# Scores of the first four attention pairs: one head's 128 queries, with 64-row matmuls for each half of the keys

## The chip, the cores and the metric

The kernel runs on one NeuronCore of a Trainium2 chip. The metric is the device time of one execution in microseconds (us); lower is better. A profile is one execution taken by the hardware profiler. Its engines are PE (TensorE matmuls), PEld (TensorE weight loads), DVE (VectorE), ACT (ScalarE), POOL (GpSimd) and SP (SyncE, which here only issues DMAs).

## What is computed

A sparse softmax attention (4 batches, 8 heads, 576 positions, head size 64) is followed by two feed-forward blocks on 2304 tokens. Everything is float32 at the borders.

```python
def _attn_ref(q, k, v, tau):                      # q, k, v: (4, 8, 576, 64)
    scale = 1.0 / np.sqrt(q.shape[-1])
    scores = scale * np.matmul(q, k.transpose(0, 1, 3, 2))
    thresh = np.max(scores, axis=-1, keepdims=True) - tau
    scores = np.where(scores >= thresh, scores, -1000000000.0)
    scores = scores - np.max(scores, axis=-1, keepdims=True)
    attn = np.exp(scores)
    attn = attn / (np.sum(attn, axis=-1, keepdims=True) + 1e-09)
    return np.matmul(attn, v)
# x = attention output as (2304, 512)
# moe:  (x @ w1) * (x @ w2) @ w3 @ w_out          # d_ff 1024
# moe2: elu(x @ w_in) @ w_out2                    # d_ff 2048
```

## The kernel before

The 32 heads are worked on as 16 pairs, and each pair as nine tiles of 128 query rows, 144 tiles in all. One tile passes through these steps: scores on PE (`emit_S`) into an `s` buffer of two PSUM banks (288 keys in each), the row maximum on DVE (`emit_max`), two tiny POOL steps for bias and threshold, the exponential on ACT (`emit_exp`), mask and row sum on DVE (`emit_mask`). Then the probabilities are transposed. Most tiles of the first four pairs do this on PE (`emit_X`, five transposes back into the same `s` buffer) with a copy by ACT (`emit_C`) into `pt`; other tiles are split into two float16 parts (`emit_H`, `emit_L`) and go through DMA transposes (`emit_T`). There are three `s` buffers, so a tile's scores wait until an earlier tile has left its buffer. The product with V (`emit_PV`) follows per group of four or five tiles, then the normalisation, for which the reciprocal row sums take a way through DRAM (`store_r`, `load_r`).

The first four pairs (`NPL = 4`, tiles 0 to 35) form their scores in plain float32; the later ones split operands into two fast float32 parts. In the plain pairs a tile holds 64 queries of the even head and 64 of the odd head. Both heads lie in one `qkp` buffer, the even one on rows 0 to 63, the odd one on rows 64 to 127, and the opposite rows of the query columns are zeros, written once by `new_plain` (eight memsets on DVE and POOL). The four matmuls of a tile contract all 128 rows with 64 stationary columns: two heads by two halves of the keys. A profile shows two records for each plain float32 matmul.

While attention runs, PE also works on the first products of the feed-forward block (`ab`), one block of 576 tokens behind, with weights that DVE, ACT and POOL unpack (`raw_w`, `u_w`, `w_w`, `W`). The order of all this is made by a planner (`Plan`): each step has an engine, a written-in duration, a key and what it depends on, and the planner simulates engines and emits each engine's instructions in the order it found. `d` in the loop over tiles is the duration of a tile's scores. On the chip each engine works in exactly that order. From about 460 us on, only feed-forward work is left, in an order that is written out by hand and untouched here.

Of the kernel before, what the change touches and what calls it, by code (L numbers as in the profile page):

```python
# [7 lines left out]
F32 = mybir.dt.float32  # L8
# [10 lines left out]
P = 128  # L19
B, H, S, D = 4, 8, 576, 64  # L20
HS = S // 2
# [123 lines left out]
def attention_moe_moe2(  # L145
# [106 lines left out]
    QW = S + D  # L252
    qkt, raw = {}, {}

    def new_plain(p, low, high):
        t = hp_.tile([P, 1792], F32, tag=f"qk{p % 2}", name=f"qkp{p}", bufs=2)
        qkt[2 * p] = qkt[2 * p + 1] = t
        low.memset(t[D:P, :S], 0.0)
        high.memset(t[:D, S:2 * S], 0.0)

    def load_plain(p, j, eng=SP):
        r = slice(j * D, (j + 1) * D)
        t = qkt[2 * p][r, j * S:3 * S].rearrange("p (x c) -> p x c", c=S)
        eng.dma_start(t[:, ::2 - j], qk[2 * p + j][r].rearrange("p (x c) -> p x c", c=S))

    def load_qk(h):
        raw[h] = rqk.tile([P, 2 * S], F32, tag="rqk", name=f"rqk{h}")
# [73 lines left out]
    def emit_S(i):  # L341
        sc[i] = s = ps_s.tile([P, 2, 512], F32, tag="s", name=f"s{i}")
        if i >= NTILE:
            return
        p, pos = SEQ[i]
        j, t = ORDER[pos]
        a, b = qkt[2 * p], qkt[2 * p + 1]
        if p < NPL:
            for n in range(2):
                k = 2 * S + n * HS  # L350
                for j, c in enumerate((pos * D, S + (pos + 1) % TPP * D)):
                    T.matmul(s[j * D:(j + 1) * D, n, :HS], a[:, c:c + D], a[:, k:k + HS], start=True, stop=True)
            return
        if j == 2:
            ops = [(a[:, 4 * P:5 * P], a), (b[:, :P], b)]
        elif j == 1:
            ops = [(b[:, (t + 1) * P:(t + 2) * P], b)]
        else:
            ops = [(a[:, t * P:(t + 1) * P], a)]
        ops = [(q, k, QW + x * S) for q, k in ops for x in range(2)]  # L360
        for n in range(2):
            for x, (q, k, c) in enumerate(ops):
                c += n * HS
                T.matmul(s[:, n, :HS], q, k[:, c:c + HS], start=(x == 0), stop=(x == len(ops) - 1))  # L364
# [50 lines left out]
    def place(i):  # L415

        p, pos = SEQ[i]
        j, t = ORDER[pos]
        o = pt[p, int(pos >= 4)]
        if p < NPL:  # L420
            c = (pos - 4 * (pos >= 4)) * P
            return o.rearrange("p c j t -> p c (j t)")[:, :, c:c + P]
        if j == 2:
            return o[:, :, :, 256:320]
        c = (t % 2) * P
        return o[:, :, j, c:c + P]

    def emit_T(i):
        p, pos = SEQ[i]
        if p >= NPL and ORDER[pos][0] == 2:  # L430
            for j in range(2):
                SP.dma_start_transpose(pt[p, 1][:, :, j, 256:320], hl[i][j * D:j * D + D, :])
        else:
            SP.dma_start_transpose(place(i), hl[i])
# [32 lines left out]
    def store_r(p, n):  # L467
        w = 4 + n
        rdr[p, n] = rdp.tile([w, P], F32, tag=f"rd{n}", name=f"rd{p}_{n}")
        if p < NPL:  # L470
            d = rdr[p, n].rearrange("t c -> (t c)").rearrange("(j t c) -> t j c", j=2, c=D)
            SP.dma_start(d, rts[p, n][:w].rearrange("t (j c) -> t j c", j=2))
        else:
            SP.dma_start(rdr[p, n], rts[p, n][:w])

    def load_r(p, n, k):
        if k == 0:
            rbc[p, n] = rbp.tile([P, 320], F32, tag="rb", name=f"rb{p}_{n}")
        o = rbc[p, n]
        if p < NPL:  # L480
            d = rdr[p, n].rearrange("t c -> (t c)").rearrange("(j o c) -> j o c", j=2, o=1)
            SP.dma_start(o[:, :NW[n]], d.to_broadcast([2, D, NW[n]]))
        elif k == 0:
            d = rdr[p, n][:4].rearrange("t c -> (t c)").rearrange("(j o c) -> j o c", j=2, o=1)
            SP.dma_start(o[:, :256], d.to_broadcast([2, D, 2 * P]))
        else:
# [5 lines left out]

    def emit_PV(p, n, part):
        w, q = NW[n], pt[p, n]
        if p < NPL:
            q = q.rearrange("p c j t -> p c (j t)").rearrange("p c (t j d) -> p c j t d", j=2, d=D)
        if part == 0:
            po_[p, n] = ps_m.tile([P, 512], F32, tag="m", name=f"pv{p}_{n}")
        if not of_dma(p, n):
            k = min(P, S - part * P)  # L500
            for j in range(2):
                T.matmul(  # L502
                    po_[p, n][j * D:(j + 1) * D, :w], vraw[p][:k, j, part * D:(part + 1) * D],
                    q[:k, part, j, :w // D if p < NPL else w], start=(part == 0), stop=(part == 4),
                )
            return
        for c, x, vc in PVC[part]:
            for j in range(2):
                x_ = q[:, c, j, :w // D if p < NPL else w]
                T.matmul(  # L510
                    po_[p, n][j * D:(j + 1) * D, :w], v16[p][:, j, x, vc * D:(vc + 1) * D], x_,
                    start=(c == 0 and x == 0), stop=(c == 8),
# [61 lines left out]


    V.memset(spread, 1.0 / VSCALE)
    for p in range(NPL):
        new_plain(p, *((V, G), (G, G), (V, V), (V, V))[p])
    for j, e in enumerate((SP, A)):
        load_plain(0, j, e)  # L580
    SP.dma_start(tau_sb, tau.to_broadcast([P, 1]))
# [20 lines left out]

    for i in range(NTILE + 4):
        p, pos = SEQ[i] if i < NTILE else (NPAIR - 1, 0)
        d = 0.05 if i >= NTILE else 1.15 if p < NPL else 1.1 if pos == 8 else 0.6
        o = S_[i] = op(call(emit_S, i), eng="PE", us=d, key=i)
        ring["s", i] = take("s", 3, o)
        if i >= NTILE:
# [40 lines left out]
    for p in range(NPL):  # L649
        QK[p] = []  # L650
        if p:
            QK[p] = [op(call(load_plain, p, j), (), "SP", 0.1, AT[p, 0] - 8, 4.0) for j in range(2)]
        for i in range(NTILE):
            if SEQ[i][0] == p:
                pl.after(S_[i], *QK[p])
# [42 lines left out]

    GRP = sorted(((p, n) for p in range(NPAIR) for n in range(2)), key=lambda g: AT[g[0], 8 if g[1] else 3])
    def load_rs(p, n):  # L700
        for k in range(1 + (n and p >= NPL)):
            load_r(p, n, k)

    pvs = []
# [438 lines left out]
```

## Time and profile before

| | us |
|---|---|
| median of three runs | 1067.16 (1064.76 to 1068.95) |
| the profiled execution, its own time | 1067.07 |
| its span, first to last instruction | 1065.0 |
| PE busy in the span | 1014.1 |
| DVE busy in the span | 583.6 |

The profile's page gives busy time by engine, then 40 equal slices of the span with the busy share of each engine in tenths. A grouped view gives, for each line of code and shape, the busy time, the mean duration of one and the idle time of that engine just before, with what ended it ("<-DVE e L394" is a wait that VectorE's line 394 ended). The view of the waits sums who waited for whom. A timeline lists instructions in order, neighbours of a kind merged.

### The profile page before, as it was taken

The page shows a single profiled execution, that of the slowest core. Times are in us where ns is not written, and L with a number is a line of the kernel's source. Part 1 is how long each engine was busy: PE and PEld are TensorE (multiplying, and loading weights), DVE is VectorE, ACT ScalarE, POOL GpSimd, SP SyncE. Part 2 cuts the span into 40 slices and gives each one's busy share as a digit, 9 for nine tenths or more (in the row PEclk, how much of TensorE's full clock was granted, in tenths as well). Part 3 has the DMA queues.
Part 4 walks back from the last instruction along what each step waited for, and adds up shares of the span by engine and source line. Part 5 has one row for each costly group of instructions (what it writes and reads, how often), then busy time and mean ns, then how long its engine had stood idle before and what let it go on. Part 6 is the DMA issues. An engine that isn't in the chain of part 4 may idle for free.

```text
span 1065.0 us, 17060 instructions
## 1 busy us (share of the span) xinstructions
PE 1014.1 (95%) x6318; PEld 887.0 (83%) x6318; DVE 583.6 (55%) x1072; ACT 514.0 (48%) x864; POOL 441.7 (41%) x586
## 2 busy tenths in 40 slices
PE   7878999979999999989999999999999999999998
PEld 4445788867888888889879999989999899899997
DVE  4788888764676666646555565843332333323322
ACT  3776777764666665534334555533232232322322
POOL 1648867765657665413321231332222222222221
PEclk8999999998999999999999999999999999999999
DMA  8227688876559444466617673300000000000000
GB/s 264 90 92 197 133 159 137 138 151 158 112 129 160 122 116 87 102 211 211 218 45 242 190 239 110 119 1 30 1 1 30 1 30 1 2 30 1 30 1 30
DMA packets 119726, 109.70 MB, mean 103 GB/s; under 512 B 88176, under 2 KB 106844, under 8 KB 115036
## 3 DMA queue, kind: packets, MB, share of 16 engines
q1 hardware_dynamic: 115532, 78.97, 31.3%
q10 hardware_dynamic: 4112, 29.66, 8.1%
q8 instruction: 49, 0.80, 0.3%
q14 instruction: 33, 0.27, 0.1%
HBM read 73.73 MB, written 14.23 MB: 83 GB/s over the span
## 4 chain that ended last, share of the span: by engine, by line
PE 58%; DMA 1%; issue 1%; POOL 1%; ACT 1%; DVE 1%; SPq 0%; POOLq 0%; ACTq 0%; DVEq 0%
PE h L1033 19%; PE o L1062 19%; PE x L1000 9%; PE ab L552 6%; PE m L860 4%; DMA rb<-rd 1%; POOL hl L405 0%; PE s L364 0%; DMA th<-g_dr 0%; PE s L442 0%; PE pv L502 0%; PE pv L510 0%; DVE sl L200 0%; POOL hl L406 0%; ACT hl L401 0%
## 5 line engine op out<-in xcount | busy, mean ns | idle before, releaser
L552 PE MATMUL ab<-x,W 128*128 128x256 f32 (+1 forms) x1536 | 232.1, 301 | 3.5 <-DVE xf L521 3.5
L552 PEld LDWEIGHTS ab<-x,W 128*128 128x128 f32 x1536 | 211.0, 190 | 10.2 <-issue 3.8
L1062 PE MATMUL o<-WO,sl 128*128 128x512 f32 x864 | 215.7, 394 | 0.6 <-POOL sl L1054 0.6
L1033 PE MATMUL h<-sl,W 128*128 128x384 f32 x1152 | 215.7, 337 | 0.0
L1033 PEld LDWEIGHTS h<-sl,W 128*128 128x128 f32 x1152 | 202.8, 188 | 8.3
L1054 POOL TENSOR_TENSOR sl<-th,sl 128x384 fp32r<-128x384 f32 x87 | 88.4, 1017 | 266.5 <-ACT sl L1049 266.5
L1062 PEld LDWEIGHTS o<-WO,sl 128*128 128x128 f32 x864 | 161.1, 188 | 30.7 <-POOL sl L1054 1.1
L1042 DVE TENSOR_SCALAR th<-h 128x384 f32<-128x384 f32 x96 | 53.3, 555 | 182.8 <-PE h L1033 182.8
L394 DVE SCALAR_TENSOR_TENSOR e<-s,st,e 128x576 f32<-128x576 f32 x144 | 115.3, 814 | 59.2 <-ACT e L388 31.3
L1043 ACT ACTIVATE th<-th 128x384 f32<-128x384 f32 x96 | 50.4, 525 | 194.5 <-DVE th L1042 194.5
L373 DVE TENSOR_REDUCE st<-s 128x1 f32<-128x576 f32 x144 | 106.0, 748 | 23.5 <-PE s L364 7.3
L1000 PE MATMUL x<-sl,M 128*128 128x384 f32 x576 | 101.1, 337 | 0.5 <-ACT sl L199 0.3
L1000 PEld LDWEIGHTS x<-sl,M 128*128 128x128 f32 x576 | 99.6, 188 | 1.9 <-DVE sl L200 0.8
L405 POOL TENSOR_TENSOR hl<-e,hl 128x512 f16<-128x512 f32 x70 | 83.1, 1188 | 24.4 <-ACT hl L401 24.1
L364 PE MATMUL s<-qk 128*128 128x288 f32 x480 | 83.8, 307 | 8.4 <-DVE e L394 4.5
L388 ACT ACTIVATE e<-s,st 128x576 f32<-128x576 f32 x108 | 77.0, 736 | 27.2 <-DVE st L373 17.0
L1049 ACT ACTIVATE sl<-th 128x384 fp32r<-128x384 f32 x96 | 50.4, 525 | 76.7 <-PE o L1062 46.5
L1047 DVE SCALAR_TENSOR_TENSOR th<-th,h 128x384 f32<-128x384 f32 x96 | 53.1, 554 | 58.2 <-ACT th L1043 58.1
L364 PEld LDWEIGHTS s<-qk 128*128 128x128 f32 x480 | 70.1, 192 | 13.3 <-issue 3.8
L442 PE MATMUL s<-ident,e 128*128 128x128 f32 (+1 forms) x370 | 56.1, 284 | 19.5 <-DVE e L394 19.2
L446 ACT ACTIVATE pt<-s 128x640 f32<-128x640 f32 x74 | 51.5, 700 | 45.0 <-PE s L442 36.1
L442 PEld LDWEIGHTS s<-ident,e 128*128 128x128 f32 (+1 forms) x370 | 38.5, 136 | 37.4 <-DVE e L394 32.4
(89 smaller groups left out, 1200.4 us busy)
## 6 DMA issues: line engine op xcount, KB each, us to landing
rqk<-in_qk SPq DMA_DIRECT2D x24, 576.0 KB
raw_wo<-in_wo ACTq DMA_DIRECT2D x12, 1024.0 KB
th<-g_dr SPq DMA_DIRECT2D x48, 192.0 KB
raw_w<-in_w SPq DMA_DIRECT2D x8, 1024.0 KB
raw_w<-in_w3t ACTq DMA_DIRECT2D x8, 1024.0 KB
raw_win<-in_win ACTq DMA_DIRECT2D x8, 1024.0 KB
vr<-in_v SPq DMA_DIRECT2D x16, 320.0 KB
g_dr<-g SPq DMA_DIRECT2D x16, 320.0 KB
```

Of the source, the lines that this page charges most:

```text
L364: T.matmul(s[:, n, :HS], q, k[:, c:c + HS], start=(x == 0), stop=(x == len(ops) - 1))
L373: V.tensor_reduce(st[i][:, 0:1], sc[i][:, :, :HS], axis=AX.XY, op=ALU.max, negate=True)
L388: A.activation(et[i], sc[i][:, :, :HS], AF.Exp, bias=st[i][:, 2:3] if by_dma(i) else st[i][:, 0:1])
L394: V.scalar_tensor_tensor(et[i], sc[i][:, :, :HS], st[i][:, 1:2], et[i], op0=ALU.is_ge, op1=ALU.mult, accum_out=sm[p][:, pos:pos + 1],)
L405: G.tensor_tensor(t[:, S + 64:], e[:, :512], t[:, :512], op=ALU.subtract)
L442: T.transpose(o[:k, c * P:(c + 1) * P], e[:, c * P:c * P + k], ident)
L552: T.matmul(o[:, :w], wf[:, m, wx, kt, :], x[:, xx, :], start=(kt == 0 and k == 0), stop=(kt == NK - 1 and k == 2),)
L1000: T.matmul(o[:, :TB], M[:, f, mx, e * P:(e + 1) * P], gh[j, f][:, gx, :], start=(k == 0), stop=(k == 23),)
L1033: T.matmul(o[:, :TB], WI[f][:, wx, kt, :], xh[j, kt][:, xx, :], start=(k == 0), stop=(k == 3 * NK - 1),)
L1042: V.tensor_scalar(t, o[:, :TB], 0.0, None, op0=ALU.min)
L1054: (V if jobs else G).tensor_tensor(x[:, 1, :], thin[2 + f % 2], f32(x[:, 0, :]), op=ALU.subtract)
L1062: T.matmul(po[j, t], gg[j, f][:, gx, t * P:(t + 1) * P], WO[f // 2][:, f % 2, wx, :], start=(f == 0 and k == 0), stop=(f == NF2 - 1 and k ...
```

## The change

For the plain pairs each head now has its own half of the `qkp` buffer. Rows 0 to 63 hold its queries and the first 288 keys, rows 64 to 127 hold the same queries again and the last 288 keys. There are no zeros and no memsets. A tile is 128 queries of one head: two matmuls, each of 64 rows by 128 stationary columns, one on the upper and one on the lower rows, each into its own PSUM bank. The ninth tile of a pair holds the last 64 queries of both heads and takes four matmuls of 64 rows by 64 columns. Tile order, `pt` layout and reciprocals thereby become those of the later pairs. A head is loaded by three DMAs instead of one, and the second head's load of pairs 1 to 3 is planned behind the first head's. `load_r` takes a second DMA for the five-tile groups, and the ninth tile of pairs 1 and 3 takes two DMA transposes. The planner's duration of the scores becomes 0.66.

```diff
-    def new_plain(p, low, high):
-        t = hp_.tile([P, 1792], F32, tag=f"qk{p % 2}", name=f"qkp{p}", bufs=2)
-        qkt[2 * p] = qkt[2 * p + 1] = t
-        low.memset(t[D:P, :S], 0.0)
-        high.memset(t[:D, S:2 * S], 0.0)
     def load_plain(p, j, eng=SP):
-        r = slice(j * D, (j + 1) * D)
-        t = qkt[2 * p][r, j * S:3 * S].rearrange("p (x c) -> p x c", c=S)
-        eng.dma_start(t[:, ::2 - j], qk[2 * p + j][r].rearrange("p (x c) -> p x c", c=S))
+        if j == 0:
+            t = hp_.tile([P, 1792], F32, tag=f"qk{p % 2}", name=f"qkp{p}", bufs=2)
+            for x in range(2):
+                qkt[2 * p + x] = t[:, x * (S + HS):(x + 1) * (S + HS)]
+        t = qkt[2 * p + j]
+        for x in range(2):
+            r = slice(x * D, (x + 1) * D)
+            if x == 0:
+                eng.dma_start(t[r], qk[2 * p + j][r, :S + HS])
+            else:
+                eng.dma_start(t[r, :S], qk[2 * p + j][r, :S])
+                eng.dma_start(t[r, S:], qk[2 * p + j][r, S + HS:])
...
         if p < NPL:
-            for n in range(2):
-                k = 2 * S + n * HS
-                for j, c in enumerate((pos * D, S + (pos + 1) % TPP * D)):
-                    T.matmul(s[j * D:(j + 1) * D, n, :HS], a[:, c:c + D], a[:, k:k + HS], start=True, stop=True)
+            if j == 2:
+                ops = [(slice(0, D), a, 4 * P, D), (slice(D, P), b, 0, D)]
+            else:
+                ops = [(slice(0, P), (a, b)[j], t * P + j * D, P)]
+            for o, x, c, m in ops:
+                for n in range(2):
+                    r = slice(n * D, n * D + D)
+                    T.matmul(s[o, n, :HS], x[r, c:c + m], x[r, S:], start=True, stop=True)
...
     def emit_T(i):
-        if p >= NPL and ORDER[pos][0] == 2:
+        if ORDER[pos][0] == 2:
...
-        d = 0.05 if i >= NTILE else 1.15 if p < NPL else 1.1 if pos == 8 else 0.6
+        d = 0.05 if i >= NTILE else 0.66 if p < NPL else 1.1 if pos == 8 else 0.6
...
-            QK[p] = [op(call(load_plain, p, j), (), "SP", 0.1, AT[p, 0] - 8, 4.0) for j in range(2)]
+            QK[p] = [op(call(load_plain, p, 0), (), "SP", 0.1, AT[p, 0] - 8, 4.0)]
+            QK[p].append(op(call(load_plain, p, 1), QK[p][:1], "SP", 0.1, AT[p, 0] - 8, 4.0))
...
     def load_rs(p, n):
-        for k in range(1 + (n and p >= NPL)):
+        for k in range(1 + n):
             load_r(p, n, k)
```

On PE, at the scores of tiles 3 to 6 before (`s3` is tile 3's score buffer, `e3` its probabilities, `qkp1` the queries and keys of pair 1, `k` a filler product, `rr` the reciprocal sums):

```order
L352 MATMUL s3_217<-qkp0_117 64x288 x4
L352 MATMUL s4_226<-qkp1_120 64x288 x4
L442 MATMUL s2_171<-ident_114,e2_215 128x128 x4
L442 MATMUL s2_171<-ident_114,e2_215 64x128
L369 MATMUL k3_252<-spread_115 128x128 x2
L369 MATMUL k4_256<-spread_115 128x128 x2
L352 MATMUL s5_263<-qkp1_120 64x288 x4
L442 MATMUL s3_217<-ident_114,e3_250 128x128 x4
```

The same place on PE after the change:

```order
L359 MATMUL s3_220<-qkp0_117 128x288 x2
L446 MATMUL s2_165<-ident_114,e2_193 128x128 x4
L446 MATMUL s2_165<-ident_114,e2_193 64x128
L376 MATMUL k3_233<-spread_115 128x128 x2
L359 MATMUL s4_246<-qkp1_144 128x288 x2
L359 MATMUL s5_255<-qkp1_144 128x288 x2
L376 MATMUL k4_259<-spread_115 128x128 x2
L376 MATMUL k5_264<-spread_115 128x128 x2
L446 MATMUL s3_220<-ident_114,e3_244 128x128 x4
```

A tile's scores are two matmuls of 128 output rows in place of four of 64, and the scores of tile 4 stand behind the transposes of tile 2.

On SP, the loads behind pair 1 and the first weight piece before (`rqk` and `vr` are later queries, keys and values, `raw_w121` the second weight piece):

```order
L264 DMA qkp2_123<-in_qk 64x2x576
L264 DMA qkp2_123<-in_qk 64x1152
L264 DMA qkp3_126<-in_qk 64x2x576
L264 DMA qkp3_126<-in_qk 64x1152
L268 DMA rqk8_161<-in_qk 128x1152
L300 DMA vr1_196<-in_v5 128x640
L300 DMA vr2_234<-in_v5 128x640
L268 DMA rqk9_242<-in_qk 128x1152
L195 DMA raw_w121_261<-in_w12 128x2048
```

The later part of the same stretch on SP after the change, from `vr1` on:

```order
L303 DMA vr1_202<-in_v5 128x640
L264 DMA qkp1_144<-in_qk 64x864
L266 DMA qkp1_144<-in_qk 64x576
L267 DMA qkp1_144<-in_qk 64x288
L264 DMA qkp2_150<-in_qk 64x864
L266 DMA qkp2_150<-in_qk 64x576
L267 DMA qkp2_150<-in_qk 64x288
L264 DMA qkp3_154<-in_qk 64x864
L266 DMA qkp3_154<-in_qk 64x576
L267 DMA qkp3_154<-in_qk 64x288
L303 DMA vr2_242<-in_v5 128x640
L271 DMA rqk9_249<-in_qk 128x1152
```

The first heads of pairs 1 to 3 are still loaded ahead of `rqk8` and `vr1`; the second heads now stand behind `vr1` and ahead of `vr2`, `rqk9` and `raw_w121`, which is the next row.

On ACT, around the values of pair 1 and the second weight piece before (`v16` is made from `vr`, `u_w` from `raw_w`):

```order
L210 ACTIVATE u_w120_224<-raw_w120_155 128x1024
L305 ACTIVATE v16_1_237,am1_236<-vr1_196 128x2x320
L386 ACTIVATE e3_250<-s3_217,st3_232,esc_111 128x576
L446 ACTIVATE pt0_0_205<-s2_171 128x5x128
L446 ACTIVATE pt0_0_205<-s3_217 128x5x128
L232 ACTIVATE W0_286<-w_w120_239 128x2x512
L465 ACTIVATE rt0_0_297<-s5_263 4x128
L386 ACTIVATE e4_300<-s4_226,st4_283,esc_111 128x576
L305 ACTIVATE v16_3_312,am3_311<-vr3_274 128x2x320
L210 ACTIVATE u_w121_321<-raw_w121_261 128x1024
```

The same on ACT after the change:

```order
L210 ACTIVATE u_w120_229<-raw_w120_148 128x1024
L450 ACTIVATE pt0_0_201<-s2_165 128x5x128
L393 ACTIVATE e3_244<-s3_220,st3_231,esc_111 128x576
L308 ACTIVATE v16_1_253,am1_252<-vr1_202 128x2x320
L450 ACTIVATE pt0_0_201<-s3_220 128x5x128
L232 ACTIVATE W0_277<-w_w120_239 128x2x512
L469 ACTIVATE rt0_0_293<-s5_255 4x128
L393 ACTIVATE e4_296<-s4_246,st4_281,esc_111 128x576
L210 ACTIVATE u_w121_311<-raw_w121_262 128x1024
```

The copy of tile 2 and the exponential of tile 3 moved ahead of the step that needs `vr1`, and the step that needs `raw_w121` no longer stands behind the one that needs `vr3`.

## Rows read from the trace of the kernel before

**Rows 1.** The page, engines: busy us, share of the span, instructions.
```profile
PE 1014.1 (95%) x6318; PEld 887.0 (83%) x6318; DVE 583.6 (55%) x1072; ACT 514.0 (48%) x864; POOL 441.7 (41%) x586
```

**Rows 2.** Four stretches: length, busy us and count by engine, granted clock, DMA share, GB/s.
```profile
0.00:24.00 24.00, 16.39 (x93) 11.22 (x95) 12.06 (x27) 8.37 (x12) 4.66 (x16) 0.94 0.94 287
24.00:124.00 100.00, 87.21 (x639) 53.94 (x636) 81.58 (x152) 71.93 (x106) 68.21 (x101) 0.98 0.41 122
124.00:460.00 336.00, 311.88 (x2422) 271.64 (x2420) 228.42 (x505) 212.02 (x366) 211.00 (x356) 0.98 0.66 132
460.00:1065.00 605.00, 598.60 (x3168) 550.21 (x3168) 261.52 (x389) 221.72 (x381) 157.87 (x115) 1.00 0.23 77
```

**Rows 3.** PE by line in 24 to 124 us: busy, mean ns, idle before.
```profile
L352 PE MATMUL s<-qkp 128*64 128x288 f32 x244 | 36.1, 424 | 2.7 <-DVE e L394 1.4 <-ACT pt L446 1.1
L442 PE MATMUL s<-ident,e 128*128 128x128 f32 (+1 forms) x115 | 17.8, 289 | 9.8 <-DVE e L394 9.8
```

**Rows 4.** Timeline of PE: start, length, line, records, idle before.
```profile
6.02 5.40 PE L352 MATMUL s<-qkp 128*64 128x288 f32 x24 [2.04 <-DMA qkp<-in_qk]
...
22.54 2.19 PE L352 MATMUL s<-qkp 128*64 128x288 f32 x8 [4.10 <-ACT pt L446]
...
31.67 1.19 PE L352 MATMUL s<-qkp 128*64 128x288 f32 x8 [0.79 <-ACT pt L446]
...
34.98 2.16 PE L352 MATMUL s<-qkp 128*64 128x288 f32 x16
```

**Rows 5.** Timeline of PE in stretches of 0.05 us: the records that run there.
```profile
34.98 0.46 PE L352 MATMUL s<-qkp 128*64 128x288 f32 x2
...
35.27 0.41 PE L352 MATMUL s<-qkp 128*64 128x288 f32 x2
...
35.51 0.41 PE L352 MATMUL s<-qkp 128*64 128x288 f32 x2
```

**Rows 6.** The whole span by line and shape: busy, mean ns, idle before.
```profile
L552 PE MATMUL ab<-x,W 128*128 128x256 f32 x768 | 103.1, 285 | 0.0
...
L352 PEld LDWEIGHTS s<-qkp 128*64 128x64 f32 x288 | 19.9, 147 | 25.6 <-ACT pt L446 8.3 <-issue 7.3 <-DVE e L394 1.6
```

**Rows 7.** Waits in 24 to 124 us: total us, times, longest.
```profile
ACT pt L446 <- PE s L442: 8.7, 6, 3.5
...
DVE e L394 <- ACT e L386: 6.7, 11, 2.4
...
ACT pt L446 <- PE pv L502: 4.4, 1, 4.4
DVE st L373 <- PE s L352: 4.4, 6, 1.6
DVE st L373 <- PE s L460: 3.7, 3, 2.2
```

**Rows 8.** Timeline of the start: ACT and POOL where they wait for loads.
```profile
20.35 0.74 ACT L305 ACTIVATE v<-vr 128x640 f16<-128x640 f32 x1 [3.73 <-DMA vr<-in_v]
...
29.49 1.14 ACT L210 ACTIVATE u_w<-raw_w 128x1024 f32<-128x1024 f32 x1
...
19.64 0.74 POOL L271 TENSOR_SCALAR rqk<-rqk,esc 128x576 f32<-128x576 f32 x1 [6.72 <-DMA rqk<-in_qk]
```

**Rows 9.** DMAs in 0 to 30 us: 40 slices of 0.75 us, busy tenths, GB/s; issues.
```profile
DMA  0038999999988999999999999999998921000000
GB/s 0 0 55 240 270 220 199 379 308 212 272 227 328 415 380 312 232 209 237 243 258 209 313 328 401 413 462 435 369 485 378 391 115 53 20 7 0 0 3 0
...
qkp<-in_qk SPq DMA_DIRECT2D x7, 288.0 KB
...
qkp<-in_qk ACTq DMA_DIRECT2D x1, 288.0 KB
```

More of the change, by code (lines that the diff above doesn't have):

```diff
@@ L419, in place @@
         o = pt[p, int(pos >= 4)]
-        if p < NPL:
-            c = (pos - 4 * (pos >= 4)) * P
-            return o.rearrange("p c j t -> p c (j t)")[:, :, c:c + P]
         if j == 2:
@@ L469, in store_r @@
         rdr[p, n] = rdp.tile([w, P], F32, tag=f"rd{n}", name=f"rd{p}_{n}")
[L470 to L474, printed above, removed]
+        SP.dma_start(rdr[p, n], rts[p, n][:w])
     def load_r(p, n, k):
@@ L479, in load_r @@
         o = rbc[p, n]
[L480 to L483, printed above, removed]
+        if k == 0:
             d = rdr[p, n][:4].rearrange("t c -> (t c)").rearrange("(j o c) -> j o c", j=2, o=1)
@@ L494, in emit_PV @@
         w, q = NW[n], pt[p, n]
-        if p < NPL:
-            q = q.rearrange("p c j t -> p c (j t)").rearrange("p c (t j d) -> p c j t d", j=2, d=D)
         if part == 0:
@@ L503, in emit_PV @@
                     po_[p, n][j * D:(j + 1) * D, :w], vraw[p][:k, j, part * D:(part + 1) * D],
-                    q[:k, part, j, :w // D if p < NPL else w], start=(part == 0), stop=(part == 4),
+                    q[:k, part, j], start=(part == 0), stop=(part == 4),
                 )
@@ L508, in emit_PV @@
             for j in range(2):
-                x_ = q[:, c, j, :w // D if p < NPL else w]
+                x_ = q[:, c, j]
                 T.matmul(
@@ L576, in attention_moe_moe2 @@
     V.memset(spread, 1.0 / VSCALE)
-    for p in range(NPL):
-        new_plain(p, *((V, G), (G, G), (V, V), (V, V))[p])
     for j, e in enumerate((SP, A)):
```

## The prediction

> **What bounds the kernel now.** I read the page first: PE is busy 1014.1 us of the span [rows 1], so an edit counts if it takes PE work away, or takes away a wait that leaves PE idle. The windows then say where PE still has air [rows 2]. From 460 us on it is busy 598.60 of 605.00 us, with code the change does not touch; that part can only start earlier. From 124 to 460 it is busy 311.88 of 336.00. The plain pairs lie before: 0 to 24 us (start, PE busy 16.39, DMA share 0.94: loads set the pace) and 24 to 124 (PE 87.21, DVE 81.58, ACT 71.93 of 100). In this second stretch no engine is full: tiles go round PE, DVE, POOL, ACT, DVE, PE, ACT with three score buffers, and each engine waits in turn. PE's own idle time there stands before the transposes, 9.8 us, ended by DVE's mask [rows 3]. DVE in turn waits for PE: 4.4 us for scores and 3.7 us for the small transposes of the reciprocals, which queue behind scores on PE; 6.7 us it waits for ACT's exponential, and ACT itself waits 8.7 and 4.4 us for PE [rows 7]. So scores are one link in a ring, neither hidden nor the only bound.
>
> **The scores, removed and added.** Two records of the old form start together and the next two 0.24 us later (35.27, 35.51) [rows 5]: the two 64-column halves of the array run side by side, one pair of records per 0.24 us. A tile has 8 records, so 4 x 0.24 = 0.97 us, plus an end of 0.22: a burst of one tile takes 1.19 us and of two tiles 2.16 [rows 4], as it should. The new tile has two matmuls, hence 4 records of the same 288 columns, one matmul on each row half. If the row halves run side by side as the column halves do, that is 2 x 0.24 = 0.49 us, alone 0.71. This saves 0.485 us on each of 32 tiles: 15.5 us. The four ninth tiles have four matmuls of 64 by 64: nothing saved if only two run together (0.97), 0.485 each if all four do; 0 to 1.9 us in all. The new weight loads have 128 columns for 64. Lower bound: hidden, as the old loads of 147 ns were [rows 6]. Upper: the block matmuls of 256 columns need 103.1 us / 768 = 134 ns with a 128-column load of their own [rows 6]; two such loads one after the other are 0.27 us for 0.24, or 0.05 us a tile, 2 us in all. I take hidden, since the old loads overlap too. PE work removed: 13.5 to 17.4 us, middle 15.5.
>
> The Trainium skill, TensorEngine Tiling (Array Packing), Key Properties, says that different tiles of the array can load weights and multiply in parallel. Rows 5 agree for column halves; no run here shows row halves. By it PE saves the 15.5 us; without it the third rival below holds.
>
> **What of it reaches the end.** In 24 to 124 us the L352 bursts take 36.1 us for 244 records, 30.5 tiles at 1.18 [rows 3]; 30.5 x 0.485 = 14.8 us of PE's 87.21 go. PE falls to 72.4, and DVE with 81.58 becomes the busiest. What was waiting for scores is shortened, the rest of the ring is not. The surest part is DVE's waits for PE, 4.4 + 3.7 = 8.1 us [rows 7]: each is at most 1.6 or 2.2 us long and stands behind a burst of one to three tiles, which shrinks by 0.5 to 1.5 us. Bounds: half of the score waits alone, 2.2 us; all of the 14.8, if ACT's waits for PE (8.7 and 4.4) shrink along. I take 8.1, since DVE cannot give more without ACT's and POOL's links getting faster. From tile 46 on, PE's order relative to the tiles is nearly the old one, so what is gained is carried to the end.
>
> **The start.** The first 24 records take 5.40 us [rows 4]; they would take half, 2.7 us less. It is not kept. The first score waited for its load at 6.02 [rows 4], and pair 0 now brings 864 KB for 576 (heads of 432 KB, formerly 288 [rows 9]): 288 KB more at 240 to 270 GB/s [rows 9] is 1.1 to 1.2 us later. Then POOL waits for `rqk` until 19.64 and ACT for `vr` until 20.35, and PE's next burst starts only at 22.54 [rows 4, 8]. Ahead of `vr1` on the queue stand now 2160 KB of queries and keys for 2304, so it lands when it did. Behind it come the three second heads, so that in total 8 x 144 = 1152 KB more are to be moved. The DMAs are busy until about slice 32, 24.8 us [rows 9]; at 200 to 480 GB/s they are so for 2.5 to 6 us longer, to 27.3 to 30.8. The second weight piece stands at the end of that queue, and ACT took it up at 29.49 [rows 8], with the copy of tile 4 and the exponentials of tiles 5 and 6 behind it. So whatever lead PE has by then waits there, and up to about 2 us more are lost: 0 to +2, I take +1.0.
>
> **Edits with one answer.** The memsets (DVE, POOL, before 5 us) lie under the first load: nothing. Two more issues a head on SP, four more DMAs of the reciprocals and two more transposes: SP waits for others through this stage, nothing; if the second reciprocal DMA came last, only the normalisation behind it would wait. The rows of POOL, ACT and DVE are re-sorted by the planner; the nearest row for a bad place in an order is the single 4.4 us wait of ACT behind a product with V [rows 7], so I allow 4.4 us either way in the range.
>
> Sum: 1067.07 - 8.1 + 1.0 = 1060.0 us. The profiled execution lies 0.1 us from the median, so the same number stands for the median.
>
> **Rivals.** (1) *The wait is replaced.* The mask and maximum on DVE (81.58 of 100) or ACT behind POOL set the pace, and PE merely idles longer before its transposes. For it: PE's idle time there is already DVE's doing [rows 3]. Against: DVE itself waits 8.1 us for PE. Gain 0 to 3, load cost 1: about 1067. The Trainium skill, same page, PSUM Bottleneck, warns of this: tiling speeds up TensorE and leaves the emptying of PSUM as it was. The trace agrees as far as DVE would be the busiest engine then.
> (2) *PE is what counts.* The planner fills PE's free time with block products earlier, and all 15.5 us are kept: 1067.1 - 15.5 = 1051.6. For it: PE's share in rows 1, and ACT's waits for PE. Against: no stretch before 124 us has PE full.
> (3) *Row halves do not run together.* Then a tile is 4 records in turn, 0.97 us as before, and a ninth tile 8 records, 1.94: 4 x 0.97 = 3.9 us more, plus 1.0 for loads: 1072.0. Nothing in the trace shows row halves.
> (4) *The loads decide, and the kernel gets slower.* The 1152 KB move at about 200 GB/s, 5.9 us; the second weight piece then lands past 30.8, ACT blocks with three tiles behind it, and the ring gives nothing back: 1067.1 + 5.9 = 1073. It decides once that piece lands later than some 2 us after 29.49. For it: that queue was full to 24.8 us. Against: seven slices in rows 9 moved more than 400 GB/s.
>
> **How the numbers follow.** Forecast 0.46 (gain 3 to 12 net), rival 1 0.24, rival 2 0.14, rival 3 0.07, rival 4 0.09. Two runs of this kernel can be told apart from about 0.5%, 5.3 us: below 1061.8 and above 1072.5. Of the forecast's 0.46 some 0.33 lie below 1061.8; with rival 2 and a little of rival 1 that is 0.48 faster. Slower: rival 4 and half of rival 3, 0.13. The rest, 0.39, is within. The range leaves out the far ends of rivals 2 and 4: 1051 to 1071.
>
> **What would show it.** Right: the score records of the new form start two at a time, 0.24 us apart, and their line has about 20 us of busy time in the plain stage; tile 36's scores come 6 to 8 us earlier; DVE's waits for scores fall to about a third; from 124 us on all stages are as long as before. Rival 1: PE's idle time before the transposes grows by what the scores lost. Rival 2: PE's idle time stays and everything is 15 us earlier. Rival 3: records one at a time. Rival 4: ACT's wait for the second weight piece appears. I am wrong altogether if the stretch from tile 36 on changes its length by more than 4 us, since then an order that I took as unchanged decides.

## The result, and the profile after

The change makes the kernel slower: a median of 1073.53 us (1067.45 to 1079.11, 16 runs) against 1067.59 (1062.05 to 1074.51, 16 runs), a ratio of 1.0060 with a 95% interval of 1.0039 to 1.0082. The forecast was 1060.0 with a range up to 1071, so sign and range both missed. The profiled execution of the changed kernel took 1070.41 us (span 1068.6), below its median, so the trace shows 3.6 us of the difference and not all 5.9.

The windows of the changed kernel, in the stretches of [rows 2] (length, busy us and count of PE, PEld, DVE, ACT, POOL, then granted clock, DMA share, GB/s):

```profile
0.00:24.00 24.00, 16.87 (x84) 12.95 (x84) 10.29 (x24) 9.90 (x14) 5.00 (x15) 0.86 0.92 243
24.00:124.00 100.00, 80.39 (x532) 49.78 (x530) 77.85 (x147) 68.38 (x104) 63.26 (x97) 0.88 0.48 144
124.00:460.00 336.00, 309.84 (x2397) 270.15 (x2399) 236.15 (x508) 213.48 (x367) 216.12 (x357) 0.98 0.64 131
460.00:1068.60 608.60, 599.70 (x3184) 550.81 (x3180) 262.86 (x389) 221.50 (x381) 157.72 (x115) 1.00 0.23 77
```

From 24 to 124 us PE is busy 80.39 us for 87.21, as a lighter score step should make it. But every other engine got less done in these 100 us too (DVE 77.85 for 81.58, POOL 63.26 for 68.21), and the granted clock is 0.88 for 0.98. The kernel has fallen behind while PE had less to do.

PE by line in the same stretch, against [rows 3] (busy us, mean ns, idle before, and what ended it):

```profile
L359 PE MATMUL s<-qkp 64*128 64x288 f32 (+1 forms) x134 | 23.8, 473 | 12.3 <-ACT pt L450 10.2 <-DVE e L401 1.6
L446 PE MATMUL s<-ident,e 128*128 128x128 f32 (+1 forms) x110 | 19.0, 313 | 7.3 <-DVE e L401 7.3
L497 PE MATMUL pv<-pt,vr 128*64 128x256 f32 (+3 forms) x100 | 16.4, 457 | 0.0
```

Scores cost 23.8 us for 36.1. In exchange PE now idles 12.3 us ahead of them, for 2.7: 10.2 us of it end with ACT's copy of the transposed probabilities (L450), the step that empties a score buffer. More than half of that is a single wait:

```profile
33.99 1.33 PE L359 MATMUL s<-qkp 64*128 64x288 f32 x4 [5.50 <-ACT pt L450]
```

The copy itself came late there, because ACT was standing still for the second weight piece (below); so these 5.50 us belong to the loads, not to the round of the tiles. A transpose takes 313 ns on average for 289, at the lower clock.

The new records one by one, from two narrow timelines of PE (start, length, line, records):

```profile
38.50 0.51 PE L359 MATMUL s<-qkp 64*128 64x288 f32 x2
...
38.50 0.76 PE L359 MATMUL s<-qkp 64*128 64x288 f32 x4
```

Two records start together: the two row halves do run side by side. A tile alone takes 0.76 us for 1.19 in [rows 4].

The waits of the changed kernel from 24 to 124 us (total us, times, longest), against [rows 7]:

```profile
PE s L359 <- ACT pt L450: 10.2, 6, 5.5
ACT pt L450 <- PE s L446: 9.6, 11, 1.8
ACT u_w L210 <- DMA raw_w<-in_w: 6.0, 1, 6.0
DVE w_w L217 <- DMA raw_w<-in_w: 5.1, 1, 5.1
DVE st L380 <- PE s L464: 2.6, 2, 2.2
DVE st L380 <- PE s L359: 1.9, 3, 1.2
```

DVE's waits for scores and for the small transposes fell from 8.1 to 4.5 us. The two long waits for `raw_w`, the second weight piece, are new: before, ACT waits 0.7 us for a weight piece in this stretch, and DVE not at all.

**Where the time went.** I cut the traces at the row maxima of single tiles on DVE; a tile's row of the timeline shows when its maximum starts. For tiles 36 and 46 of the changed kernel:

```profile
124.39 0.74 DVE L380 TENSOR_REDUCE st<-s 128x1 f32<-128x576 f32 x1
...
155.69 0.72 DVE L380 TENSOR_REDUCE st<-s 128x1 f32<-128x576 f32 x1
```

In this way, for the profiled executions (us; e2 and so on are the experiments below, and the last maximum of a stretch opens the next):

| stretch | before | after | e2 | e3 | e6 | e7 | e9 | e12 |
|---|---|---|---|---|---|---|---|---|
| start to tile 9 | 38.2 | 41.3 | 40.8 | 38.6 | 36.7 | 35.8 | 39.5 | 41.9 |
| tile 9 to 36 | 85.9 | 83.1 | 85.2 | 83.0 | 89.5 | 85.8 | 87.4 | 89.1 |
| tile 36 to 46 | 23.2 | 31.3 | 30.2 | 31.3 | 23.4 | 24.8 | 23.8 | 23.2 |
| tile 46 to 75 | 81.2 | 77.6 | 77.7 | 77.4 | 79.0 | 85.1 | 82.6 | 79.7 |
| tile 75 to the end | 836.5 | 835.3 | 838.3 | 838.3 | 838.6 | 835.7 | 836.4 | 837.2 |

Before to after that is +3.1, -2.8, +8.1, -3.6, -1.2, together +3.6. The start loses, the plain tiles gain a little, and the largest single item is a stretch right behind the plain pairs that no edit touches directly.

One trace is one execution, and the first two rows of the table scatter. e6, e9 and e12 have the same loads, and the same order of DVE, ACT and POOL, yet their tile 9 comes at 36.7, 39.5 and 41.9 us. A difference of a few us in these rows shows where to look; the medians decide what it is worth. The stretch from tile 36 to 46 is steadier: 23.2 to 23.8 us in before, e6, e9 and e12, and 30.2 to 31.3 in after, e2 and e3. Its windows, first before, then after:

```profile
124.10:147.30 23.20, 23.14 (x190) 19.45 (x190) 18.54 (x43) 17.02 (x31) 15.79 (x28) 1.00 0.83 139
```

```profile
124.40:155.70 31.30, 28.47 (x216) 21.96 (x214) 25.96 (x53) 21.54 (x37) 25.22 (x36) 1.00 0.81 149
```

Before, PE is busy 23.14 of 23.20 us there. After, between the same two tiles, there is more work on every engine: DVE 25.96 for 18.54, POOL 25.22 for 15.79, PE 28.47 for 23.14. The order put it there. One of the steps that slid in is POOL's last weight conversion of this group (L235, timelines of POOL, first before, then after):

```profile
113.66 2.38 POOL L235 TENSOR_TENSOR W<-w_w,W 128x1024 fp32r<-128x1024 f32 x1
```

```profile
134.05 2.39 POOL L235 TENSOR_TENSOR W<-w_w,W 128x1024 fp32r<-128x1024 f32 x1
```

In DVE's order the eight conversion steps (`join`, L224) stood behind tiles 3, 7, 11, 13, 18, 21, 26, 30 and now stand behind 3, 7, 12, 16, 20, 26, 30, 37. With the scores' duration at 0.66 for 1.15, the planner believes that tiles go round faster, and more of them fit between two conversions.

The start is the load queue. ACT's timeline of the changed kernel:

```profile
32.20 1.14 ACT L210 ACTIVATE u_w<-raw_w 128x1024 f32<-128x1024 f32 x1 [6.03 <-DMA raw_w<-in_w]
```

ACT stands still for 6.03 us for the second weight piece, which in [rows 8] it took up at 29.49. SP, timeline of the DMA issues, before:

```profile
17.94 0.33 SPq L195 DMA_DIRECT2D raw_w<-in_w  x1
```

and after:

```profile
22.42 0.54 SPq L267 DMA_DIRECT2D qkp<-in_qk  x1
23.00 0.58 SPq L303 DMA_DIRECT2D vr<-in_v  x1
23.63 0.43 SPq L271 DMA_DIRECT2D rqk<-in_qk  x1
24.19 0.34 SPq L195 DMA_DIRECT2D raw_w<-in_w  x1
```

The piece is issued 6.25 us later, since the second heads of pairs 1 to 3 (nine DMAs) stand ahead of it. PE idles meanwhile, and a window of 24 to 38 us, first before, then after, shows the clock:

```profile
24.00:38.00 14.00, 11.88 (x74) 7.03 (x71) 9.58 (x19) 9.98 (x15) 7.52 (x13) 0.87 0.27 95
```

```profile
24.00:38.00 14.00, 6.16 (x29) 4.63 (x28) 6.86 (x12) 5.52 (x10) 4.90 (x7) 0.53 0.70 253
```

PE is busy 6.16 of 14 us for 11.88, and the granted clock is 0.53 for 0.87, mostly the 1.2 GHz level.

### The profile page after: what moved, and what is told of

Read it like the earlier page. It is cut to its first block, busy times and chain, and to the rows that moved or that the text cites. A ratio compares the mean times of both kernels' runs of the same rounds, so it can differ in the third digit from the quotient of the medians.

```text
span 1068.6 us, 16815 instructions
## 1 busy us (share of the span) xinstructions
PE 1006.8 (94%) x6190; PEld 883.7 (83%) x6190; DVE 587.1 (55%) x1067; ACT 513.3 (48%) x864; POOL 442.1 (41%) x583
## 4 chain that ended last, share of the span: by engine, by line
PE 57%; DMA 1%; issue 1%; ACT 1%; DVE 1%; POOL 1%; SPq 0%; ACTq 0%; DVEq 0%; POOLq 0%
PE h L1027 19%; PE o L1056 19%; PE x L994 9%; PE ab L547 6%; PE m L854 4%; DMA rb<-rd 1%; PE s L371 0%; PE s L446 0%; DMA th<-g_dr 0%; POOL hl L412 0%; PE pv L497 0%; PE pv L505 0%; DVE sl L200 0%; DMA rd<-rt 0%; DVE st L380 0%
## 5 line engine op out<-in xcount | busy, mean ns | idle before, releaser
L547 PEld LDWEIGHTS ab<-x,W 128*128 128x128 f32 x1536 | 211.0, 190 | 10.2 <-DVE xf L516 3.9
L412 POOL TENSOR_TENSOR hl<-e,hl 128x512 f16<-128x512 f32 x70 | 85.2, 1216 | 26.2 <-ACT hl L408 25.8
L395 ACT ACTIVATE e<-s,st 128x576 f32<-128x576 f32 x108 | 77.7, 735 | 35.8 <-DVE st L380 26.8
L371 PE MATMUL s<-qk 128*128 128x288 f32 x480 | 85.9, 311 | 6.3 <-DVE e L401 3.0
L446 PE MATMUL s<-ident,e 128*128 128x128 f32 (+1 forms) x370 | 58.7, 294 | 18.1 <-DVE e L401 17.8
L446 PEld LDWEIGHTS s<-ident,e 128*128 128x128 f32 (+1 forms) x370 | 40.7, 141 | 35.7 <-DVE e L401 29.3
L450 ACT ACTIVATE pt<-s 128x640 f32<-128x640 f32 x74 | 51.4, 699 | 37.2 <-PE s L446 32.1
```

The source lines that it names most:

```text
L395: A.activation(et[i], sc[i][:, :, :HS], AF.Exp, bias=st[i][:, 2:3] if by_dma(i) else st[i][:, 0:1])
L412: G.tensor_tensor(t[:, S + 64:], e[:, :512], t[:, :512], op=ALU.subtract)
L446: T.transpose(o[:k, c * P:(c + 1) * P], e[:, c * P:c * P + k], ident)
L547: T.matmul(o[:, :w], wf[:, m, wx, kt, :], x[:, xx, :], start=(kt == 0 and k == 0), stop=(kt == NK - 1 and k == 2),)
```

## The experiments

Every kernel was timed in five rounds beside the kernel before (medians of 1067.6 to 1069.0 us in these sessions); ratios are to that, with a 95% interval; a ratio is not quite the quotient of the two medians (for e3 that would be 1.0012). The theories: **P**, the re-sorted order costs the time; **L**, the loads do; **O**, both of them do, and the new form by itself still gains; against these **N**, the new form itself costs; **W**, what PE saves is waited for again; **C**, it is lost to the half clock.

**e1: the planner's old duration, in the changed kernel.**

```diff
-        d = 0.05 if i >= NTILE else 0.66 if p < NPL else 1.1 if pos == 8 else 0.6
+        d = 0.05 if i >= NTILE else 1.15 if p < NPL else 1.1 if pos == 8 else 0.6
```

> The changed kernel with the planner's old duration of the plain scores, 1.15 for 0.66; matmuls and loads are the new ones. In the order of VectorE the joins of the eight weight pieces then stand behind tiles 3, 7, 12, 16, 16, 22, 26, 31 (changed kernel 3, 7, 12, 16, 20, 26, 30, 37; before 3, 7, 11, 13, 18, 21, 26, 30). Theory P (the planner's faster clock slides the weight conversion behind later tiles and its price is paid after tile 36): 1066 to 1069, 5 to 7 us below the changed kernel, with the stretch from the maximum of tile 36 to that of tile 46 at 23 to 26 us for 31.3. Theory L (the extra load bytes ahead of the second weight piece cost it): no change from the changed kernel, 1072 to 1075.

1074.33 us, ratio 1.0047 (1.0017 to 1.0076): no better. The old number does not give the old order, because the second head's loads now depend on the first's: conversions behind tiles 3, 7, 12, 16, 16, 22, 26, 31. The stretch from tile 36 to 46 takes 28.0 us, and that from 9 to 36 takes 93.8. "The old duration mends it" fell; the order had to be tested apart from the loads.

**e2: the planner's new duration, in the kernel before.** The reverse edit of e1, so the old form in the new order.

> The kernel before with the planner's new duration, 0.66 for 1.15; matmuls, zeros and loads are the old ones, and the engines' orders of weight pieces and blocks relative to the tiles become those of the changed kernel. Theory P: slower than before, 1072 to 1078, with the weight joins late (the eighth behind tile 37) and the stretch from tile 36 to 46 at about 30 us. Theory L: as before, 1066 to 1069, since no byte is added.

1070.88 us, ratio 1.0023 (1.0000 to 1.0046). The order alone costs the old form some 2.5 us by the ratio and 3.3 by the medians, with an interval that begins at no change. Its trace has the long stretch: 30.2 us from tile 36 to 46, without one new matmul. So that stretch belongs to the order and not to the form.

**e3: the loads of two second heads behind the second weight piece.** In the loop over the conversions of the changed kernel:

```diff
         conv[f] = [hi, lo]
+        if f == 1:
+            for p in (2, 3):
+                pl.after(QK[p][1], ld)
```

> The changed kernel with the loads of the second heads of pairs 2 and 3 moved behind the second weight piece on the queue; everything else unchanged. Theory L: ScalarE's 6.0 us wait for the second weight piece falls to 2 us or less, tile 7's maximum comes at 32 to 34 us for 36.2, and the time falls by 2 to 4 us, to 1069 to 1071. Theory P: the wait falls too, but the lead is lost again at the later weight pieces, and the time stays at 1072 to 1075.

1068.87 us, ratio 1.0004 (0.9976 to 1.0031), which no longer overlaps the interval of the change. ACT has the second piece at 29.40 and tile 9 comes at 38.6 us for 41.3. The place of two loads was worth some 4.7 us of median.

**e4: e1 and e3 together.**

> Both edits: the planner's old duration and the later loads, with the new matmuls. Theory P: as with the old duration alone, or 1 to 3 us less, 1063 to 1068. Theory L: as with the later loads alone, 1069 to 1071. If the new matmuls are worth the 8.1 us of the prediction once nothing is in their way, 1060 to 1062.

1074.77 us, ratio 1.0072 (1.0040 to 1.0103). A miss: the loads bring nothing on top of e1, so what they cost is not the same in every order. In its profile GpSimd waits long for another load (waits, 20 to 40 us):

```profile
POOL rqk L274 <- DMA rqk<-in_qk: 9.4, 1, 9.4
```

Whether that is the cause in the timed runs too was not tried.

**e5: the old order exactly, with the new form and new loads.** e1, and the second head's load without its dependency; conversions and feed-forward products then stand where they stood before.

```diff
-            QK[p].append(op(call(load_plain, p, 1), QK[p][:1], "SP", 0.1, AT[p, 0] - 8, 4.0))
+            QK[p].append(op(call(load_plain, p, 1), (), "SP", 0.1, AT[p, 0] - 8, 4.0))
```

> The changed kernel with the planner's duration for a plain tile back at 1.15 and without the rule that a pair's second-head load comes after its first: the weight conversions and the Gram work then stand where they stood in the kernel before (joins behind tiles 3, 7, 11, 13, 18, 21, 26, 30), so what is left of the change is the new matmul form and the new loads. Theory O (the re-sorted order cost about 3 us and the loads about 4, the form itself gains 4 to 5): second weight piece still at 32, tile 36 at 122 to 125, the stretch from tile 36 to tile 46 back at 23 to 25 us, and 1066 to 1069. Rival N (the new form itself is what costs, by filling less of PE and drawing a lower granted clock): the stretch stays at 28 us or more, and the time at 1072 or more.

1078.04 us, ratio 1.0101 (1.0072 to 1.0131). The stretch from tile 36 to 46 is back at 23.4 us, as O and P had it, but the time is far off O's: tile 9 comes only at 44.6 us, and from there to tile 36 it takes 91.1.

**e6: e5 with the loads of e3**, so the new form in the old order, nearly without the price of its loads.

> The kernel of e5 with the second-head loads of the third and fourth pair queued behind the second weight piece, as in e3: the new matmul form alone, in the old order and nearly without the price of its loads. Theory O: ACT has the second weight piece at about 29.5, tile 36 at 119 to 122, the stretch to tile 46 at 23 to 25 us, and 1061 to 1065, ahead of the kernel before by 3 to 6 us. Rival N: 1068 or more, since neither order nor loads were the cause. Rival W (what PE saves is waited for again, whatever the order): 1066 to 1069.

1070.73 us, ratio 1.0034 (1.0013 to 1.0055), 7.3 us ahead of e5: the loads again. But here order and loads are mended (tile 9 at 36.7, tile 36 to 46 in 23.4), and the kernel is still not faster than before. In its trace the stretch from tile 9 to 36 takes 89.5 us for 85.9, with a third of PE's work on scores gone. Where that went, the transposes of e6 from 24 to 126 us show:

```profile
L446 PE MATMUL s<-ident,e 128*128 128x128 f32 (+1 forms) x111 | 19.2, 317 | 14.6 <-DVE e L401 14.6
```

PE idles 14.6 us ahead of them, for 9.8 in [rows 3], until DVE's mask is done. O fell, and so did every explanation by order and loads alone, as far as loads can be mended here: the extra bytes of pair 0 and of the second head of pair 1 still come first.

**e7: the conversions earlier in the new order.** e3 with the planner's spacing of conversions at 4.0 tiles.

```diff
-C0, CG = 2.0, 5.5
+C0, CG = 2.0, 4.0
```

> e3 (the changed kernel, planner's new duration, second-head loads of two pairs later) with the planner's spacing of the weight conversions 4.0 tiles in place of 5.5: joins behind tiles 3, 6, 10, 14, 18, 21, 26, 30 in place of 3, 7, 12, 16, 20, 26, 30, 37. Nothing else is asked for. Theory P (the conversions that slid past tile 30 are what lengthens the stretch from tile 36 to tile 46): the eighth conversion on GpSimd ends near 115 in place of 131, tile 36 comes later by what DVE now does ahead of it (124 to 126), the stretch falls from 31 to 23 to 26 us, and the time is 1064 to 1067. If the slide is only a bookkeeping of the same work (rival): tile 46 at 152 to 154 again and 1068 to 1070, with tile 36 later by as much as the stretch is shorter.

POOL's last conversion starts at 110.80 us, tile 36 to 46 takes 24.8 us, as P had it. But 1070.78 us, ratio 1.0024 (1.0002 to 1.0045): what this stretch gave, the next took, 85.1 us from tile 46 to 75 for 77.4 in e3. The long stretch is work in another place, not work added; only the sum counts.

**e8: the conversions earlier from the start.** e3 with `C0` at -8.

> e3 with the planner's first due time of the weight conversions ten tiles earlier (-8 in place of 2) at the old spacing: joins behind tiles 3, 6, 8, 11, 14, 19, 25, 30. The early tiles then carry more of DVE's and ACT's weight work than in any other kernel here. Theory P: tile 16 some 4 to 6 us later than in e3 (63 to 65), tile 36 at 123 to 127, the stretch to tile 46 at 23 to 26, and 1064 to 1068. Rival (the early stage is bound by DVE, ACT and PE together, so work moved there costs as much as it saves later): tile 46 at 153 or later and 1069 or more.

1070.25 us, ratio 1.0011 (0.9993 to 1.0030). Tile 36 to 46 in 23.1 us, but tile 16 comes at 66.4 for 59.0 in e3. The rival is nearer.

**e9: idle matmuls against the half clock.** e6 with the fillers that stand behind the first nine tiles (two matmuls of 128 by 128) put behind all plain tiles.

```diff
-NKB = 9
+NKB = 36
...
-            kb = op(call(keep_busy, i), [o], "PE", 0.25, i + 500)
+            kb = op(call(keep_busy, i), [o], "PE", 0.02, i + 500)
```

> The kernel of e6 (new matmul form, loads late, the old order) with the two idle 128x128 matmuls that already stand behind the scores of the first nine tiles put behind those of tiles 9 to 35 too, at a planner's price so small that no other instruction moves. They write to the small PSUM banks and nobody reads them. Theory C (what PE's shorter scores save is given back, because PE idles and the granted clock goes to half, 17 us of it between 57 and 119 us in e6, so that transposes, PV and Gram products take longer): granted clock 58 to 124 back to 0.95 or more from 0.87, tile 36 at 122 to 124 in place of 126, and 1065 to 1068 in place of 1070.7. Rival W (the ring of waits from engine to engine sets the pace, the clock only follows): tile 36 at 126 or later although the clock is up, 1070 to 1073. Rival F (the fillers themselves take PE's and the banks' time): tile 36 at 128 or later and 1073 or more.

1069.12 us, ratio 1.0004 (0.9979 to 1.0029). Windows of e6 and, below it, of e9:

```profile
58.00:124.00 66.00, 54.69 (x362) 35.31 (x363) 50.89 (x95) 44.42 (x67) 46.66 (x69) 0.87 0.47 131
```

```profile
58.00:124.00 66.00, 56.16 (x401) 36.83 (x400) 53.85 (x98) 46.36 (x69) 48.77 (x70) 0.95 0.50 142
```

The clock rose from 0.87 to 0.95 and all engines got a little more done (DVE 53.85 for 50.89); the intervals of the two ratios overlap. Tile 36 came at 126.9 us, where W had it; the time lies between the forecasts of C and W.

**e10 and e11: the same fillers in e7 and, as a control, in the kernel before.**

> The kernel of e7 (new form, loads late, planner's new duration, weight conversions 4.0 tiles apart) with the same idle matmuls behind tiles 9 to 35. Theory C: clock 58 to 124 at 1.0 from 0.98, little to win there, but the drop at 26.5 and 57.2 us goes: tile 36 at 120 to 122, 1067 to 1070 in place of 1070.8. Rival F: tile 36 at 124 or later and 1072 or more.

> The control: the kernel before with the same idle matmuls behind tiles 9 to 35, nothing else moved. Its granted clock is full there already (1.00 from 58 to 124), so what it loses is the price of the fillers alone. Theory C: 0 to 3 us slower, 1067 to 1071. Rival F: 4 us or more slower, tile 36 at 128 or later.

e10 took 1070.58 us, ratio 1.0019 (0.9995 to 1.0043), against 1070.78 without; e11 1070.29, ratio 1.0005 (0.9978 to 1.0033). The fillers cost the old kernel nothing that can be told, and bring e7 nothing. In e9 and e11 no other step moved; in e10 the order of all engines changes from some 137 us on, so it is the weaker test. The profiled execution of e11, 1077.08 us, lies far above its median. Theory C in the strong form, that a full clock gives the gain back, is not borne out.

**e12: the score matmuls twice.** e6, and from tile 9 on each plain tile's scores are computed a second time into the same place.

```diff
-            for o, x, c, m in ops:
+            for o, x, c, m in ops * (1 + (i >= NKB)):
```

> The kernel of e6 (new form, loads late, the old order), with the score matmuls of tiles 9 to 71 issued twice over, the second time with the same result: PE gets back about what the change took from it (0.5 us a tile, some 30 us in all, 13 of it before tile 36) on the very path of the scores. Theory W+C (between tiles 9 and 36 the pace is set by the round from DVE over ACT and GpSimd and back, and PE's time counts only through the clock): tile 36 at 124 to 128 against 126.2 in e6, the clock 58 to 124 at 0.95 or more, 1068 to 1073. Rival S (the scores are on the path, and the gain of the form is real but is lost to something else): tile 36 at 132 or later and 1077 or more.

The text above has the size wrong: plain tiles end at 35, so it is not 30 us but what the score line shows over the span, first e6, then e12:

```profile
L359 PE MATMUL s<-qkp 64*128 64x288 f32 (+1 forms) x160 | 31.9, 515 | 10.2 <-ACT pt L450 6.5 <-DMA qkp<-in_qk 2.1 <-DVE e L401 1.5
```

```profile
L359 PE MATMUL s<-qkp 64*128 64x288 f32 (+1 forms) x284 | 43.4, 459 | 14.3 <-ACT pt L450 10.5 <-DMA qkp<-in_qk 2.3 <-DVE e L401 1.3
```

That is 11.5 us more on the path of the scores, nearly what the change had taken away. The time: 1071.95 us, ratio 1.0024 (1.0004 to 1.0045), against 1070.73 and 1.0034 (1.0013 to 1.0055) for e6. From tile 9 to 36 it took 89.1 us for 89.5. Tile 36 at 131.0 us lies between what W+C and S forecast, but tile 9 was already 5.2 us later than in e6, with nothing changed ahead of its own scores; the time is W+C's, and S fell. One thing moved along: the window of e12 below, against that of e6 above, has the clock at 0.97 for 0.87.

```profile
58.00:124.00 66.00, 57.32 (x442) 38.31 (x443) 52.23 (x95) 44.43 (x65) 45.63 (x64) 0.97 0.48 137
```

So e12 added score work and gave back clock at once. Against e9, where the clock is up too (0.95) by fillers that nobody waits for, the doubled scores cost 2.8 us of median for 11.5 us of work, with intervals that overlap. By these medians score work between tiles 9 and 36, added or removed, has a price of a small part of its own length.

**e13 and e14: two attempts to beat both.** The fillers in e3, and e9 with conversions 4.0 tiles apart.

> The kernel of e3 (the change with the loads of two pairs later, else untouched, 1068.9) with the idle matmuls behind tiles 9 to 35 that e9 had. If clock and pace are as e9 showed (1.6 us gained over e6): 1066 to 1069, granted clock 0.985 or more over the span in place of 0.98. If the fillers cost what they bring here (as in e10, where they brought 0.2): 1068 to 1071.

> An attempt at a version ahead of both: the kernel of e9 (new form, old planner duration, loads late, fillers) with the weight conversions 4.0 tiles apart (joins behind tiles 3, 6, 10, 13, 16, 21, 26, 29), earlier than in any old order but with the rest of the order kept. If an early end of the weight conversions is what the stretch behind tile 36 wants, 1063 to 1067; if the order of the first 36 tiles has nothing more to give, 1068 to 1071.

e13 took 1071.94 us, ratio 1.0030 (1.0008 to 1.0052); e14 1073.85, ratio 1.0058 (1.0036 to 1.0080). Both missed, and no version was found that beats the kernel before; e3 and e9 equal it. The trace of e13 (its fastest execution, with PE's order changed from some 117 us on) says it once more: with the granted clock at 1.00 it has the shortest way from tile 9 to 36 of all, 82.0 us, and then needs 35.5 us to tile 46. In e14 POOL's last conversion starts at 114.91 us, well before tile 36 (130.5), and the stretch still takes 28.0 us; so late conversions alone do not explain a long stretch.

**What W looks like in the trace.** The windows from tile 9 to tile 75, long enough to take in what the orders displace, of before, after, e6 and e12:

```profile
38.20:228.50 190.30, 174.61 (x1325) 130.76 (x1322) 152.57 (x312) 136.86 (x220) 139.04 (x216) 0.99 0.64 136
```

```profile
41.30:233.30 192.00, 169.80 (x1233) 126.86 (x1229) 155.09 (x311) 136.10 (x220) 140.46 (x216) 0.96 0.65 136
```

```profile
36.70:228.60 191.90, 169.59 (x1237) 127.86 (x1234) 151.40 (x312) 136.37 (x220) 138.29 (x216) 0.96 0.61 136
```

```profile
41.90:234.00 192.10, 176.82 (x1357) 134.79 (x1355) 150.59 (x312) 136.51 (x220) 137.48 (x216) 0.99 0.62 136
```

PE's busy time goes from 169.59 to 176.82 us, the length stays at 190.3 to 192.1. (Over all the traces it ranges more widely, from 188.9 us in e8 to 201.3 in e14.) The plain part of it, from tile 9 to 36, shows where the saved time goes:

| tile 9 to 36, us | before | e2 | after | e6 | e9 | e12 |
|---|---|---|---|---|---|---|
| PE busy with scores | 30.0 | 30.1 | 20.5 | 21.4 | 20.2 | 32.4 |
| PE idle ahead of scores | 1.8 | 3.0 | 6.8 | 2.5 | 3.4 | 2.1 |
| PE idle ahead of transposes | 8.9 | 4.1 | 5.0 | 13.7 | 8.3 | 8.5 |
| granted clock | 1.00 | 1.00 | 0.94 | 0.90 | 0.96 | 0.98 |

No engine is full there (before, PE is busy 75.23 and DVE 71.86 of 85.9 us), so the length is set by how steps wait for one another. In the old order (before against e6) PE's saved time turns into idle time ahead of the transposes, until DVE's mask is done; with the scores doubled (e12) that goes away again, and the length stays. In the new order (e2 against after) it turns into idle time ahead of the scores, most of it until ACT's copy is done. Where PE idles most (e6) the clock is lowest, and part of the saving never shows as less busy time: the scores fall by 9.5 us between before and after, PE's busy time up to tile 75 by 4.8. Which link of the round holds the tiles back, DVE's mask, ACT's copy or one ahead of them, was not tried.

## Why the prediction was wrong, step by step

- **The scores term** was right. Over the span the line has 160 records and 30.1 us, for 288 records of 44.9: 14.8 us less, for the 15.5 forecast. The two pairs of a tile end 0.25 us apart (0.51 and 0.76), where 0.24 was forecast, and a tile alone takes 0.76 in place of 0.71. Rival 3 is refuted: row halves run side by side. In the ninth tiles all four 64 by 64 matmuls do: four records start together, and such a tile takes 0.71 us, so the upper end of what was allowed for them came true.
- **"What of it reaches the end"**, -8.1 us, is the step that failed first. It counted DVE's waits for PE as time that the kernel gets back. Those waits did shrink by 3.6 us, but a wait that ends earlier brings time only if its engine is then not waiting for another. Here PE itself waited in their place. In the old order with loads mended (e6) the stretch from tile 9 to 75 was 1.6 us longer, not 8.1 shorter, and e12 shows that score work has little price there. This is rival 1: e6 has its sign, PE's idle time ahead of the transposes up from 8.9 to 13.7 us between tiles 9 and 36. In the changed kernel, whose order is another, the idle time came ahead of the scores instead, 6.8 us for 1.8, where ACT's copy frees a buffer. The Trainium skill, TensorEngine Tiling (Array Packing), PSUM Bottleneck, says that tiling leaves the emptying of PSUM as it was. In this order the trace agrees: between tiles 9 and 36, 4.7 us end with the copy, for 2.7 in e2 and 0.3 before.
- **The start**, +1.0, was mis-sized: tile 9 came 3.1 us later in the trace, and e3 got 4.7 us of median back by moving two loads. The bytes were right, but ACT took the piece at 32.20 us, past the upper end of 30.8 (of the slices in [rows 9] six, not seven, are over 400 GB/s). Above all, the price of ACT and DVE both standing still behind it (6.03 and 5.11 us), with PE mostly at half clock, was put at 2 us at most. Rival 4's threshold, some 2 us past 29.49, was met, and its 1073 is near the time measured, though loads are only part of it.
- **The orders**, taken as nothing with 4.4 us in the range, were the largest item of the trace: +8.1 us from tile 36 to 46, -3.6 up to tile 75. The net is some 2.5 to 3.3 us by e2, at the edge of the noise. That PE's order from tile 46 on is nearly the old one fits the trace from tile 75 on (-1.2 us); what lay between tiles 36 and 46 was not looked at.
- **The signs to look for.** Tile 36 was to come 6 to 8 us earlier and came 0.3 later. From tile 36 on the kernel changed by 3.3 us in sum, inside the 4 that I had named, but only since +8.1 met -4.8.

Loads, by e3, some 4.7 us of median, and order, by e2, some 3.3, together 8.0; the change costs 5.9. That the two simply add up is not shown. If they do, the form gives back some 2 us in the new order (e3 is 2.0 us below e2, with intervals that overlap). In the old order it gives none: e6 is above the kernel before, e9 level with it. Whether the form by itself is worth anything is left open.

## What to carry to other kernels

In a stretch where no engine is full and tiles go from engine to engine round a ring of few buffers, price a shorter step by when its engine's next step can start (its buffer free, the other engine's result there), not by the waits of the engine behind it. Doubling the step is a cheap way to see whether it has any price at all, if the clock is compared along with the time. A number that a planner reads is an edit of its own: run the old code with the new number before believing that the order costs nothing. When a change adds small DMAs ahead of a large load on one queue, look at who stands still for the large one, and before putting a wait down to a buffer, look at what the engine that frees it was waiting for.

## What the runs showed of the hardware

- Row halves of PE run two plain float32 matmuls of 64 contracted rows side by side: records start in pairs, 0.76 us for a tile of 2 x 288 columns. Four of 64 rows by 64 columns run together as well: records start in fours, 0.71 us for eight.
- The granted clock and the time scatter together from run to run. Over 32 runs of the kernel before, the mean clock ran from 0.979 to 0.992, and a higher one went with a shorter time (correlation -0.83, 0.86 us for each 0.001; in the other three sets of 23 to 29 runs -0.52 to -0.78). Which of the two causes the other is not shown. Between kernels this does not hold: e9 has a mean of 0.989 over 12 runs and e3 0.981, at the same time.
- A clock drop in the plain pairs can cost as much as this change. e11 is the kernel before up to tile 9, yet in its profile PE stood idle for 2.38 us up to 43.03 us, and was at half clock for 10.2 us from 42.5 us on, though busy for 9.67 of them: 16 score records took 4.11 us there, and 2.16 at 37.09 us. Tile 9 came 4.1 us later than before, and tile 12 8.2 us (56.9 for 48.7).
